# A convolution by short transforms: half of the first two products issued earlier, three bank pairs instead of four, row blocks in order

## The chip, the cores and the metric

The kernel runs on one core of one Trainium2 chip. The metric is device time in microseconds (us) of one execution. A core has these engines: TensorE (PE, matrix products into the accumulator memory PSUM; the loads of its stationary operand are shown as PEld), VectorE (DVE), ScalarE (ACT), GpSimd (POOL), and SyncE (SP), which here only issues transfers. Each engine works through its own list in order; semaphores order the lists among each other. PSUM has eight banks of 512 float columns.

## The reference

A convolution of width 3 along a sequence, from 1024 to 1024 channels, then a normalization with fixed mean and variance, then silu. Two sequences of 2048 positions, everything in bfloat16.

```python
B, S, C, K = 2, 2048, 1024, 3
xp = jnp.pad(x, ((0, 0), (1, 1), (0, 0)))
y = sum(jnp.einsum('bsc,cd->bsd', xp[:, k:k + S, :], w[k]) for k in range(K))
y = (y - mean) * (g * (1.0 / jnp.sqrt(var + 1e-5))) + b
return y * sigmoid(y)
```

## The kernel before

**Tiling.** Six output positions (R = 6) at a time are computed by eight products instead of eighteen. A block of eight inputs is transformed into eight points (NJ = 8); for each point, the transformed input is multiplied with a transformed weight; the eight results are combined into six rows. Points 0 and 7 (zero and infinity) use the raw taps 0 and 2 of w, the points in pairs (1, 2), (3, 4), (5, 6) use tiles u0, u1, u2 that POOL makes. A sequence has NB = 342 blocks; they are the columns of the products.

**Transforming the input.** x comes in 17 windows of 128 positions, each with the data of 21 blocks (WT = 21; the last has 6). PE multiplies a window, as stationary operand, with a constant matrix `rm` (for window 0 with `rm0`, a shifted copy that `first_matrix` makes through PSUM). One `t_job` (L322) does up to three of the eight channel tiles of two neighbouring windows: matmuls of 8 x 21 = 168 columns into two neighbouring banks, then one cast of both banks into `T_sb` in bfloat16, on ACT (L333) or on DVE (L335). Eight channel tiles take three jobs a pair of windows: tiles 0 to 2 and 3 to 5 (six matmuls, a cast of 128x1008 each), and 6 and 7 (four matmuls, 128x672). With the job of the 6-block window, which comes first (job 0), a sequence has 25 jobs. A planner in the Python code, which keeps a clock for each engine with a fixed cost and a cost per column, gives each cast to ACT or DVE, whichever would end first by its reckoning. `ahead` issues all jobs of the first sequence, on bank pairs 0, 2, 4, 6 in turn. `order` is the order of the windows: 16, then 2 to 15, then 0 and 1.

**Transfers.** SP's queue carries the windows of the first sequence in this order, with three half-width loads of w after the sixth, ninth and last window (`W0_AT`), then the second sequence's windows. There are 12 window buffers, so from the 13th window on a load waits for a job to release one.

**Units.** The work after that is 16 units, one for each of the 8 groups of 128 output channels and each sequence, on four banks each (0 to 3, then 4 to 7, and so on in turn). A product of a unit is eight matmuls, one for each channel tile, of 342 columns (L368). The first unit (`run_first`) multiplies points 0 and infinity first: product (3, 0), which is point 0 into bank 3, and (0, 7), point 7 into bank 0. Each needs all of `T_sb` for its point; ACT copies the results to `ends`. Then come points 1, 3, 2, 4, 5, 6. Between the matmuls of the first unit, `Between` issues the jobs of the second sequence at the counts of matmuls listed in `at`, on bank pairs 4-5, 6-7 and 1-2 in turn. Job q of this sequence uses `(4, 6, 1)[q % 3]`.

**The other units.** They multiply the inner points first; points 0 and 7 of a unit are added at the end (`first`, `last`), among the products of the next unit, each with the silu of one row (rows 0 and 5, L391). `silu_inner` does the four inner rows in two instructions. `rest` lists these three pieces with the place behind which each is issued. Where weights for a later unit are prepared, ACT also doubles a tile (`double_w`, L157) at the end of the unit. The results go to `yT`, are transposed by transfers and stored.

**Warm-up.** Before the first window is there, PE multiplies zeros (L74), `WARM` matmuls of 512 float columns.

Of the kernel before, what the change touches and what calls it, by code (L numbers as in the profile page):

```python
# [15 lines left out]
P = 128  # L16
R = 6
NJ = 8
W0_AT = (5, 8, 16)
EARLY = 23  # L20
XBUFS = 12
T_FIRST = 21500.0
WARM = 2
WT = 21

@with_exitstack
def kernel(
# [10 lines left out]
    nc = tc.nc  # L38
    B, S, C = x.shape
    D = w.shape[2]  # L40
    CT, DC = C // P, D // P
    NB = -(-S // R)
    NW = -(-NB // WT)
# [21 lines left out]
    ps = pspool.tile([P, 8, 512], FP32, name="ps")  # L65
    T_sb = [tpool.tile([P, CT, NJ, NB], BF16, name=f"T_sb{bi}") for bi in range(B)]
# [41 lines left out]
    clock = {"pe": 3500.0, "act": 0.0, "dve": 0.0, "dma": 3600.0}  # L108
# [3 lines left out]
    def ends(e, size):  # L112
        return max(clock[e], clock["pe"] + 100.0) + cost[e][0] * size + cost[e][1]
# [1 line left out]
    def busy(e, size):  # L115
        clock[e] = ends(e, size)

    order = [NW - 1] + list(range(2, NW - 1)) + [0, 1]
    xwin = {}

    def load_x(bi, wi):
# [86 lines left out]
    def prepare_first(dc):  # L208


        w0, w2 = raw[dc][:, 0], raw[dc][:, 2]
        g, f = (spool.tile([P, CT, P], BF16, name="w1x2") for _ in range(2))
        nc.gpsimd.tensor_scalar(f, w0, 4.0, 0.0, op0=ALU.mult, op1=ALU.add)
        for q, t, h in ((0, w0, w2), (1, g, w0)):
            if q:
                nc.gpsimd.tensor_scalar(g, w2, 4.0, 0.0, op0=ALU.mult, op1=ALU.add)
            sums[dc, q] = epool.tile([P, CT, P], FP32, name=f"e{q}")
            nc.gpsimd.tensor_tensor(sums[dc, q], t, h, op=ALU.add)

        def left():  # L220
            transform_w(dc, 0, (0,))
            double_w(dc, nc.scalar)
            transform_w(dc, 1, (0,))
            transform_w(dc, 0, (1,))
            transform_w(dc, 1, (1,))
            sums[dc, 2] = epool.tile([P, CT, P], FP32, name="e2")
            nc.gpsimd.tensor_tensor(sums[dc, 2], f, w2, op=ALU.add)
            transform_w(dc, 2)

        return left  # L230
# [40 lines left out]
    rm0 = consts.tile([P, NJ, WT], BF16, name="rm0")  # L271

    def first_matrix():

        v = ps[0:P - 1, 1, 256:256 + NJ * WT]
        nc.tensor.matmul(v, lhsT=ident[:, 1:P], rhs=rm.rearrange("p j n -> p (j n)"), start=True, stop=True)
        nc.scalar.copy(rm0[0:P - 1].rearrange("p j n -> p (j n)"), v)

    def params():

# [33 lines left out]
    def t_job(job, bank):  # L314
        wins, dst, n, c0, nct = job
        nb, size = len(wins), nct * NJ * n
        clock["pe"] = max(clock["pe"], wins[-1][1], bank_free.get(bank, 0.0))
        src = ps[:, bank:bank + nb, 0:size]
        v = src.rearrange("p b (c j n) -> p b c j n", j=NJ, n=n)
        for q, (xw, _, mat, rows) in enumerate(wins):  # L320
            for c in range(nct):
                nc.tensor.matmul(  # L322
                    v[:, q, c], lhsT=xw[0:rows, (c0 + c) * P:(c0 + c + 1) * P], rhs=mat[0:rows, :, 0:n],
                    start=True, stop=True,
                )
        dst = dst.rearrange("p c j (b n) -> p (c j) b n", b=nb)
        src = src.rearrange("p b (q n) -> p q b n", n=n)
        clock["pe"] += nb * size / 2.3
        e = min(("act", "dve"), key=lambda k: ends(k, nb * size))
        busy(e, nb * size)  # L330
        bank_free[bank] = clock[e] + 100.0
        if e == "act":
            nc.scalar.copy(dst, src)  # L333
        else:
            nc.vector.tensor_copy(dst, src)  # L335
# [8 lines left out]
    class Unit:  # L344
# [12 lines left out]
            self.low, self.mid, self.high = (ps[:, b0 + q:b0 + q + 2, lo:hi] for q in range(3))  # L357
            self.yT = yts[bi]

        def product(self, q, j, add, between):  # L360
            dc = self.dc
            nsl = slice(self.lo, self.hi)
            for ct in range(CT):
                if j == 0 or j == NJ - 1:
                    lhsT = raw[dc][:, 0 if j == 0 else 2, ct]
                else:
                    lhsT = wts[dc, (j - 1) // 2][:, (j - 1) % 2, ct]
                nc.tensor.matmul(  # L368
                    self.bank[q], lhsT=lhsT, rhs=T_sb[self.bi][:, ct, j, nsl],
                    start=not add and ct == 0, stop=ct == CT - 1, skip_group_check=add,  # L370
                )
                clock["pe"] += (self.hi - self.lo) / 2.35
                between()

        def copy(self, q, dst=None, by=None):
# [40 lines left out]
        def run_first(self, between, left, following):  # L416


            b0, b1, b2, b3 = self.bank
            sd = dpool.tile([P, 2, NB], FP32, name="sd")  # L420
            t = dpool.tile([P, 4, NB], FP32, name="t02")
            t0, t2 = t[:, 0:2], t[:, 2:4]
            ends = dpool.tile([P, 2, NB], FP32, name="ends")
            self.y23 = t1 = ypool2.tile([P, 2, NB], FP32, name="t1")
            left()
            self.product(3, 0, False, between)
            self.copy(3, dst=ends[:, 0])
            self.product(0, NJ - 1, False, between)
            self.copy(0, dst=ends[:, 1])
            clock["pe"] = max(clock["pe"], T_FIRST)  # L430
            self.product(3, 1, False, between)
            pa = self.copy(3)
            self.product(0, 3, False, between)
            pb = self.copy(0, by=4.0)
            self.product(3, 2, True, between)
            self.copy(3, dst=sd[:, 0])
            self.combine(sd[:, 1], pa, 2.0, b3, ALU.subtract)
            self.product(0, 4, True, between)
            self.combine(b1, b0, -2.0, pb)
            for d, a in ((t0, -0.0125), (t2, -0.2), (t1, -0.05)):  # L440
                self.combine(d, self.low, a, sd)
            nc.vector.tensor_tensor(t[:, 0::3], t[:, 0::3], ends, op=ALU.add)
            busy("dve", 2 * NB)
            first, second, third, fourth = following
            first()
            self.product(2, 5, False, between)
            pc = self.copy(2)
            between.rest()
            self.product(2, 6, True, between)
            self.combine(b3, b2, -0.5, pc)  # L450
            self.combine(self.low, self.high, -1.6, t0)
            self.combine(t1, self.high, -0.4, t1)
            self.combine(self.high, self.high, -0.1, t2)
            second()
            self.prepare = third, fourth
# [9 lines left out]
        def rest(self, between, last=5, first=6):  # L465


            return [
                (min(last, 5), self.silu_inner), (last, lambda: self.last(between)),
                (first, lambda: self.first(between)),  # L470
            ]

        def run(self, between, also=(), prepare=None, alone=False):

# [111 lines left out]
        if i in W0_AT:  # L586
            load_w(0, (0, 2, 1)[W0_AT.index(i)], 0)

    left = []

    def ahead(jobs, job_n):
        for job in jobs:
            t_job(job, job_n % 4 * 2)
            if job_n == 0:
                first_matrix()
            if job_n == 2:
                params()
            if job_n == 5:
                scales()
                left.append(prepare_first(0))  # L600
            job_n += 1

    ahead(t_jobs(0), 0)
# [5 lines left out]
    class Between:  # L609


        n = done = 0
        jobs = list(t_jobs(1))
        at = [8, 12, 14, 16, 18, 20, 22] + [22 + (6 * CT - 22) * (q + 1) // (EARLY - 7) for q in range(EARLY - 7)]

        def do(self):
            t_job(self.jobs[self.done], (4, 6, 1)[self.done % 3] if self.done < EARLY else (6, 4)[(self.done - EARLY) % 2])
# [11 lines left out]
    between = Between()  # L629
    seq = [(dc, bi) for dc in range(DC) for bi in range(B)]  # L630
    late = [nc.sync] * (S // R // P + 1) + [nc.gpsimd]
    before = prev = None
    for i, (dc, bi) in enumerate(seq[:-1]):
        unit = Unit(dc, bi, i % 2 * 4)
        if i == 0:
            unit.run_first(between, left[0], prepare_second(1))
        else:
            unit.run(
                between,
                prev.rest_first() if i == 1 else  # L640
                prev.rest(between, *((4, 5) if i >= len(seq) - 3 else (5, 4) if i == 2 else (5, 6))),
                2 if i == 2 else dc + 2 if bi == 1 and 0 < dc < DC - 2 else None,
                i == 1,
            )
        if i == 0:
            xwin_scope.close()
            olast = ctx.enter_context(tc.tile_pool(name="olast", bufs=3))
            wpools[1] = ctx.enter_context(tc.tile_pool(name="wpool1", bufs=1))
        if i in (0, 4, 8):
            for k in range(3):  # L650
                load_w(i // 4 + 1, k)
        if i == len(seq) - 2:
            prev.turn(olast, ((1, R), (0, 1)))
        elif prev:
            prev.turn()
        if before:
            before.store(late if i == len(seq) - 2 else ())
        before, prev = prev, unit
    before.store(late)
    dc, bi = seq[-1]  # L660
# [45 lines left out]
```

## Time and profile before

| | before |
|---|---|
| times of three runs | 188.25, 188.66, 190.04 us |
| profiled execution, its own time | 188.5 us |
| its span, first to last instruction | 186.7 us |
| PE busy | 177.0 us (95%), 1402 matmuls |
| DVE busy | 154.9 us (83%) |
| POOL busy | 146.1 us (78%) |
| ACT busy | 111.9 us (60%) |
| x and w reads, output writes | 14.82 MB read, 8.39 MB written |
| granted TensorE clock | 0.998 of full speed, mean of the span |

The page counts an instruction as busy from its start to its modelled end; PE's matmuls overlap, so the distance from one to the next is shorter than the duration given for one. Idle time is put down to what ended it ("<-DMA xw": a window of x arrived). "Issue" is time in which an engine waited for nothing that the profile shows.

### The profile page before, as it was taken

To read this page: it belongs to the slowest core of one execution; us is meant where nothing else is said; L and a number is where in the kernel's file an instruction comes from. 1 tells how busy PE (TensorE), PEld (TensorE's weight loads), DVE (VectorE), ACT (ScalarE), POOL (GpSimd) and SP (SyncE) were. 2 spreads that over 40 slices of the span, in tenths; PEclk is the share of its full clock that TensorE was granted. 3 is DMA by queue.
4 is the path that set the end of the run, shared out by engine and by line. 5 is a ranking of instruction groups with operands and counts; after the bars stand their busy time and mean duration, and the time that the engine had idled before them with its cause. 6 is when DMAs were issued, how large, how long until landed. Compare 5 with 4: busy or idle time off the path is not lost.

```text
span 186.7 us, 3721 instructions
## 1 busy us (share of the span) xinstructions
PE 177.0 (95%) x1402; PEld 125.0 (67%) x1402; DVE 154.9 (83%) x213; ACT 111.9 (60%) x182; POOL 146.1 (78%) x86
## 2 busy tenths in 40 slices
PE   6879999999999999999999999999999999999980
PEld 2658688776666666666666666666666666669980
DVE  5549667897979999999988998879988996769681
ACT  3789698689465565456545654565455555454790
POOL 3477999989998879999999999999999971021031
PEclk9999999999999999999999999999999999999999
DMA  5999999057607455798749667978596577979725
GB/s 168 315 351 334 381 388 232 4 151 193 123 4 142 102 109 130 196 187 198 150 109 210 115 136 201 202 178 167 115 199 117 123 79 163 181 140 167 162 62 112
DMA packets 86958, 31.72 MB, mean 170 GB/s; under 512 B 73542, under 2 KB 82778, under 8 KB 86940
## 3 DMA queue, kind: packets, MB, share of 16 engines
q1 hardware_dynamic: 85820, 31.24, 72.5%
q10 hardware_dynamic: 864, 0.21, 0.5%
q8 instruction: 11, 0.18, 0.4%
q0 software_dynamic: 256, 0.03, 0.2%
q14 instruction: 7, 0.06, 0.1%
HBM read 14.82 MB, written 8.39 MB: 124 GB/s over the span
## 4 chain that ended last, share of the span: by engine, by line
PE 83%; DMA 4%; DVE 4%; ACT 2%; SPq 2%; issue 1%; ACTq 0%; DVEq 0%
PE ps L368 77%; PE ps L322 5%; DVE T_sb L335 4%; DMA xw<-in_x_dram 3%; SPq L125 2%; DMA rows<-in_g_dram 1%; ACT yT L391 1%; ACT T_sb L333 1%; PE ps L534 1%; SPq L141 0%; ACTq L70 0%; DVEq L701 0%; ACT pc L379 0%; DVE sd L386 0%; DVE o L535 0%
## 5 line engine op out<-in xcount | busy, mean ns | idle before, releaser
L368 PE MATMUL ps<-T_sb,u 128*128 128x342 bf16 (+2 forms) x816 | 120.1, 299 | 0.5 <-ACT yT L391 0.5
L368 PEld LDWEIGHTS <-u 128*128 128x128 bf16 x816 | 76.7, 97 | 33.7 <-issue 0.7
L190 POOL TENSOR_TENSOR u<-e,w1x 128x1024 bf16<-128x1024 f32 x32 | 69.4, 2194 | 3.9 <-DVE e L171 2.5
L368 PE MATMUL ps<-T_sb,wch 128*128 128x342 bf16 (+2 forms) x272 | 43.0, 299 | 0.4 <-ACT T_sb L333 0.4
L391 ACT ACTIVATE yT<-ps,beta,scale 128x342 bf16<-128x342 f32 (+4 forms) x49 | 33.8, 721 | 11.9 <-PE ps L368 11.9
L190 POOL TENSOR_TENSOR u<-e,wch 128x1024 bf16<-128x1024 f32 x16 | 38.6, 2434 | 1.9 <-DMA wch<-in_w_dram 1.3
L386 DVE SCALAR_TENSOR_TENSOR t<-ps,sd 128x684 f32<-128x684 f32 (+2 forms) x51 | 39.1, 822 | 0.6
L368 PEld LDWEIGHTS <-wch 128*128 128x128 bf16 x272 | 25.6, 97 | 11.7 <-issue 0.7
L379 ACT COPY pc<-ps 128x342 f32<-128x342 f32 (+2 forms) x34 | 14.5, 427 | 30.1 <-PE ps L368 30.0
L335 DVE CAST T_sb<-ps 128x1008 bf16<-128x1008 f32 (+2 forms) x20 | 22.0, 1121 | 11.4 <-PE ps L322 11.2
L333 ACT CAST T_sb<-ps 128x1008 bf16<-128x1008 f32 (+2 forms) x30 | 24.9, 866 | 6.8 <-PE ps L322 6.6
L386 DVE SCALAR_TENSOR_TENSOR ps<-ps,t 128x684 f32<-128x684 f32 (+2 forms) x34 | 28.3, 832 | 0.6
L171 DVE SCALAR_TENSOR_TENSOR e<-wch 128x1024 f32<-128x1024 bf16 x12 | 27.2, 2263 | 0.0
L322 PE MATMUL ps<-rm,xw 128*128 128x168 bf16 (+2 forms) x272 | 24.8, 233 | 2.4 <-DMA xw<-in_x_dram 1.9
L322 PEld LDWEIGHTS <-xw 128*128 128x128 bf16 (+2 forms) x272 | 20.2, 97 | 8.3 <-DMA xw<-in_x_dram 3.0
L386 DVE SCALAR_TENSOR_TENSOR ps<-ps,pc 128x342 f32<-128x342 f32 (+2 forms) x34 | 16.8, 496 | 8.6 <-PE ps L368 7.5
L169 POOL TENSOR_TENSOR e<-wch 128x1024 f32<-128x1024 bf16 x7 | 16.9, 2409 | 0.0
L391 ACT ACTIVATE yT<-t,beta,scale 128x684 bf16<-128x684 f32 (+2 forms) x17 | 15.7, 926 | 0.0
L386 DVE SCALAR_TENSOR_TENSOR t<-ps,t 128x684 f32<-128x684 f32 (+2 forms) x17 | 13.9, 818 | 0.0
L576 POOL DMA_DIRECT2D out_dram<-o x2 | 1.4, 710 | 15.6 <-DMA o<-yT 15.6
L379 ACT COPY sd<-ps 128x342 f32<-128x342 f32 (+2 forms) x17 | 7.3, 429 | 9.7 <-PE ps L368 8.8
L381 ACT ACTIVATE pc<-ps 128x342 f32<-128x342 f32 (+2 forms) x17 | 7.5, 440 | 9.1 <-PE ps L368 6.8
(52 smaller groups left out, 61.3 us busy)
## 6 DMA issues: line engine op xcount, KB each, us to landing
xw<-in_x_dram SPq DMA_DIRECT2D x32, 256.0 KB
out_dram<-o SPq DMA_DIRECT2D x28, 192.0 KB
wch<-in_w_dram SPq DMA_DIRECT2D x9, 512.0 KB
out_dram<-o SPq DMA_DIRECT2D x14, 120.0 KB
wch<-in_w_dram SPq DMA_DIRECT2D x6, 256.0 KB
out_dram<-o SPq DMA_DIRECT2D x3, 128.0 KB
o<-yT SPq DMA_TRANSPOSE x15
out_dram<-o SPq DMA_DIRECT2D x12, 7.5 KB
```

Of the source, the lines that this page charges most:

```text
L125: nc.sync.dma_start(out=xw[0:hi - lo, :], in_=x[bi, lo:hi, :])
L169: eng.tensor_tensor(e, w0, w2, op=ALU.add)
L171: eng.scalar_tensor_tensor(out=e, in0=f, scalar=4.0, in1=h, op0=ALU.mult, op1=ALU.add)
L190: nc.gpsimd.tensor_tensor(wts[dc, q][:, i], sums[dc, q], o, op=(ALU.add, ALU.subtract)[i])
L322: nc.tensor.matmul(v[:, q, c], lhsT=xw[0:rows, (c0 + c) * P:(c0 + c + 1) * P], rhs=mat[0:rows, :, 0:n], start=True, stop=True,)
L333: nc.scalar.copy(dst, src)
L335: nc.vector.tensor_copy(dst, src)
L368: nc.tensor.matmul(self.bank[q], lhsT=lhsT, rhs=T_sb[self.bi][:, ct, j, nsl], start=not add and ct == 0, stop=ct == CT - 1, skip_group_che ...
L379: nc.scalar.copy(dst, self.bank[q])
L381: nc.scalar.mul(dst, self.bank[q], by)
L386: nc.vector.scalar_tensor_tensor(out=out, in0=in0, scalar=scalar, in1=in1, op0=ALU.mult, op1=op1)
L391: nc.scalar.activation(self.yT[:, rows, self.lo:self.hi], src, ACT.Silu, bias=beta[:, dc:dc + 1], scale=scale[:, dc:dc + 1])
```

## The change

- `order`: windows 16, 0, 1, ..., 15, for both sequences.
- `first_matrix` goes ahead of job 0; its copy is made by DVE instead of ACT. One warm-up matmul instead of two.
- From job 13 of the first sequence on, the jobs use the bank pairs 4-5, 6-7, 1-2 in turn (`(4, 6, 1)[job_n % 3]`); up to job 12, 0, 2, 4, 6 in turn as before.
- The first eight windows in order make up the first 168 columns, complete with job 12. Products (3, 0) and (0, 7) of the first unit are computed for these columns between jobs 13 and 18: six matmuls after job 13 and two after job 15 for the one, five after job 16 and three after job 18 for the other. `run_first` computes the other 174 columns where it computed 342.
- The second sequence's jobs 1 to 6 come at other counts of matmuls.
- `rest`: where the place of `first` comes before the places of the other two, the list is turned round. That holds in the third unit alone, where the last product and row 5's silu of the second unit now come ahead of its inner silus.
- `T_FIRST`, a lower bound for the planner's clock, goes from 21500 to 21000.

```diff
-T_FIRST = 21500.0
-WARM = 2
+T_FIRST = 21000.0
+HALF = 8
+WARM = 1
...
-    order = [NW - 1] + list(range(2, NW - 1)) + [0, 1]
+    order = [NW - 1] + list(range(NW - 1))
...
-        nc.scalar.copy(rm0[0:P - 1].rearrange("p j n -> p (j n)"), v)
+        nc.vector.tensor_copy(rm0[0:P - 1].rearrange("p j n -> p (j n)"), v)
...
-        def product(self, q, j, add, between):
+        def product(self, q, j, add, between, cols=None, cts=range(CT), part=None):
+
             dc = self.dc
-            nsl = slice(self.lo, self.hi)
-            for ct in range(CT):
+            nsl = cols or slice(self.lo, self.hi)
+            dst = ps[:, self.b0 + q, nsl]
+            for ct in cts:
...
                 nc.tensor.matmul(
-                    self.bank[q], lhsT=lhsT, rhs=T_sb[self.bi][:, ct, j, nsl],
-                    start=not add and ct == 0, stop=ct == CT - 1, skip_group_check=add,
+                    dst, lhsT=lhsT, rhs=T_sb[self.bi][:, ct, j, nsl],
+                    start=not add and part != 1 and ct == cts[0], stop=part != 0 and ct == cts[-1],
+                    skip_group_check=add,
                 )
-                clock["pe"] += (self.hi - self.lo) / 2.35
+                clock["pe"] += (nsl.stop - nsl.start) / 2.35
...
-            self.product(3, 0, False, between)
+            late = slice(HALF * WT, NB)
+            self.product(3, 0, False, between, late)
             self.copy(3, dst=ends[:, 0])
-            self.product(0, NJ - 1, False, between)
+            self.product(0, NJ - 1, False, between, late)
...
                 (first, lambda: self.first(between)),
-            ]
+            ][::1 if first >= min(last, 5) else -1]
...
-    left = []
+    left, one = [], Unit(0, 0, 0)
+    half = {
+        13: (3, 0, (3, 4, 5, 6, 7, 0), 0), 15: (3, 0, (1, 2), 1),
+        16: (0, NJ - 1, (3, 4, 5, 6, 7), 0), 18: (0, NJ - 1, (0, 1, 2), 1),
+    }
 
     def ahead(jobs, job_n):
         for job in jobs:
-            t_job(job, job_n % 4 * 2)
             if job_n == 0:
                 first_matrix()
+            t_job(job, job_n % 4 * 2 if job_n < HALF // 2 * 3 + 1 else (4, 6, 1)[job_n % 3])
...
+            if job_n in half:
+                q, j, cts, part = half[job_n]
+                one.product(q, j, False, lambda: None, slice(0, HALF * WT), cts, part)
             job_n += 1
...
-        at = [8, 12, 14, 16, 18, 20, 22] + [22 + (6 * CT - 22) * (q + 1) // (EARLY - 7) for q in range(EARLY - 7)]
+        at = [8, 16, 16, 16, 20, 21, 22] + [22 + (6 * CT - 22) * (q + 1) // (EARLY - 7) for q in range(EARLY - 7)]
```

More of the change, by code (lines that the diff above doesn't have):

```diff
@@ L633 @@
     for i, (dc, bi) in enumerate(seq[:-1]):
-        unit = Unit(dc, bi, i % 2 * 4)
+        unit = Unit(dc, bi, i % 2 * 4) if i else one
         if i == 0:
```

## The prediction

> **What bounds the kernel now.** I read the busy time by stretch first, to see where TensorE (PE) is short of work at all. Columns: stretch, its length, then busy us and instructions of PE, PE's weight loads, VectorE (DVE), ScalarE (ACT), GpSimd (POOL); clock, DMA share, GB/s.
>
> ```profile
> 9.00:13.49 4.49, 2.86 (x32) 2.25 (x33) 2.33 (x3) 4.01 (x6) 3.49 (x7) 1.00 1.10 349
> 13.49:19.31 5.82, 5.24 (x61) 4.48 (x62) 4.92 (x5) 5.21 (x8) 4.36 (x4) 1.00 1.10 340
> 19.31:38.20 18.89, 18.62 (x193) 14.92 (x193) 13.50 (x15) 14.08 (x21) 18.73 (x10) 1.00 0.74 237
> 38.20:181.00 142.80, 142.34 (x1062) 98.62 (x1061) 127.91 (x166) 83.11 (x142) 115.28 (x55) 1.00 0.72 147
> ```
>
> From 38.20 to 181.00 PE idles for 0.46 us in 142.8. So whatever shifts the start of that stretch shifts the end by as much, and nothing there gives it back. Up to 13.49 PE waits for x windows (DMA share about 1). From 13.49 to 19.31 it is neither full nor starved by DMA; DVE and ACT are busy there for 4.92 and 5.21 us of 5.82. The chain of waits (start, length, work) says who sets the pace:
>
> ```profile
> 14.35 0.93 DVE T_sb L335
> ...
> 16.73 0.61 PE ps L322 x6
> 17.34 0.02 issue
> 17.36 1.91 ACT T_sb L333 x2
> ...
> 19.31 1.44 PE ps L368 x8
> ...
> 30.86 1.22 DVE T_sb L335
> 32.09 0.04 issue
> 32.13 0.61 PE ps L322 x6
> 32.74 0.02 issue
> 32.76 1.21 DVE T_sb L335
> ```
>
> At 14 to 19 us the casts of transformed windows out of PSUM carry the chain, then the first product. At 30.86 the reader sees the row that matters most below: a DVE cast, PE refilling the same pair of banks, the next DVE cast. From cast to cast that is 32.76 - 30.86 = **1.90 us**. It is the period whenever a DVE cast and its refill alternate on one pair. The timeline of single instructions gives the unit prices.
>
> ```profile
> 13.49 0.61 PE L322 MATMUL ps<-rm,xw 128*128 128x168 bf16 x6 [0.30 <-DMA xw<-in_x_dram]
> 14.35 1.21 DVE L335 CAST T_sb<-ps 128x1008 bf16<-128x1008 f32 x1 [1.58 <-PE ps L322]
> 18.61 1.21 DVE L335 CAST T_sb<-ps 128x1008 bf16<-128x1008 f32 x1
> 19.15 0.74 ACT L333 CAST T_sb<-ps 128x672 bf16<-128x672 f32 x1
> 19.31 0.60 PE L368 MATMUL ps<-T_sb,wch 128*128 128x342 bf16 x3 [0.45 <-ACT T_sb L333]
> ```
>
> One 168-column record alone lasts 0.25, six 0.61: a step of (0.61 - 0.25)/5 = 0.072 us. One 342-column record lasts 0.31, three 0.60: a step of 0.145. The casts of job 14 and job 23 are those at 14.35 and 18.61: three pairs of windows in 4.26 us, 1.42 a pair.
>
> **The start.** One warm-up matmul less frees PE about 1.85 us earlier (four records of warm-up in 3.71 us). The first matrix goes ahead of job 0, its copy moves from ACT (0.30) to DVE (between that and the 0.56 of a 384-column DVE cast); DVE is idle from 3.64 to 6.61. Row blocks 0 and 1 merely change places with others in the load order; sizes and queue stay. All of it lies before 9.59, where PE has waited 0.96 us for the seventh window. I take 0; if that window came at once, the cover were gone and the gain at most 0.96.
>
> A rule of the Trainium skill speaks against the missing warm-up: "TensorE: Matmul & The Clock Gate", Part 1, says that the array runs at half clock until it has been busy for about 3.4 us. The profile shows a granted clock of 1.00 from the first slice on, so no run here shows that state at the start.
>
> **The sixteen half products.** The diff issues 16 matmuls of 168 columns between jobs 13 and 18, and leaves 16 of 174 columns where there were 16 of 342. The later cost falls from 0.145 to 0.145 x 174/342 = 0.074 each, 16 x 0.071 = 1.14 us off the path. In front, 61 matmuls x 0.072 = 4.4 of the 5.82 us after 13.49 are needed, so 1.4 us is free for 16 x 0.072 = 1.15. By PE's time alone they fit. But their results stay in banks 0 and 3, and that is the price:
>
> **The ring of three.** From job 13 on, jobs go round three bank pairs (4-5, 6-7, 1-2) instead of four. A pair of windows is also three jobs. So the first job of each pair always meets banks 6-7, the second banks 1-2, the third 4-5. The planner's arithmetic (fixed plus per-column cost, earliest end wins), carried through with the diff's terms, gives ACT, DVE, ACT for each of the last four pairs; for the kernel before, the same arithmetic gives exactly the engines in the trace. So DVE casts jobs 14, 17, 20, 23, all in banks 1-2: the 1.90 us cycle. PE, in order, waits for those banks, and all later jobs queue behind it.
>
> Job 14 is ready after the six half products of job 13: 14.35 + 6 x 0.072 = 14.79. Then 16.69, 18.59, 20.49, and the last cast ends at 20.49 + 1.21 = 21.70; before, 18.61 + 1.21 = 19.82. **1.88 us later.** Nothing else is slower than 1.90 a pair: ACT needs 1.51 (0.90 + 0.61 from start to start), PE at most 21 x 0.072 = 1.51, the windows came in for 1.42 a pair.
>
> Now the first product. Channel tiles 0 to 2 can go at 20.58, when job 24's matmuls are issued; tile 3 waits for job 23's cast, 21.75; five steps of 0.074 give 22.12. Before, it ended at 20.69: +1.43. From there to the unit's third product it takes 0.32 (job 0) + 1.16 (jobs 1 to 3) in both, plus 8 x 0.145 = 1.16 before and 0.59 after. Net at that point: 1.43 - 0.57 = **+0.86**.
>
> The bounds: if the ring costs nothing and only the 0.44 of half products delays the casts, 0.44 - 1.02 = -0.58, where 1.02 = 1.88 - 0.86 is what the shorter products return. If PE's and ACT's queueing adds a tenth to each cycle, 3 x 0.19 more, +1.43. I take +0.86, because the 1.90 row is this very pattern.
>
> **The second sequence's jobs.** Jobs 1 to 3 now come in one bunch at the 16th matmul, jobs 4 to 6 at the 20th to 22nd. Carrying on with the same durations, job 4 waits 0.16 us for job 1's banks (DVE cast until 24.88), job 7 0.10, job 8 0.07: **+0.33**, bounds 0 and 0.66 (all covered; each twice as long). ACT's doubling of w1, at 19.76 before, shifts behind the later casts; POOL needs its result two tiles ahead of PE, which leaves over 2 us of cover; without that it would cost the 1.9 us of the shift. The x loads that wait for released windows go out up to 1 us later; their queue was full until 29 us, so this is hidden.
>
> **Row 5's silu first in the third unit.** This takes away PE's only stall after 38 us:
>
> ```profile
> 53.88 0.96 ACT L391 ACTIVATE yT<-t,beta,scale 128x684 bf16<-128x684 f32 x1
> 54.74 1.44 ACT L391 ACTIVATE yT<-ps,beta,scale 128x684 bf16<-128x684 f32 x2
> 56.06 1.06 ACT L157 ACTIVATE w1x<-wch 128x1024 bf16<-128x1024 bf16 x1
> 57.59 0.45 ACT L379 COPY pc<-ps 128x342 f32<-128x342 f32 x1 [0.47 <-PE ps L368]
> 56.23 5.97 PE L368 MATMUL ps<-T_sb,u 128*128 128x342 bf16 x40 [0.46 <-ACT yT L391]
> ```
>
> PE could go on at 54.44 + 8 x 0.145 = 55.60 and goes on at 56.23: 0.63 to gain. But ACT now idles until row 5's product is done, 54.64, and everything behind moves back: row 5 until 55.16, the two inner silus (0.86, 0.81 from start to start) until 56.83, the doubling until 57.79, and only then the copy of the next unit's first product, done at 58.24. The product that adds into that bank would start at 55.60 + 16 x 0.145 = 57.92 and waits until 58.28. **0.63 - 0.36 = -0.27**; bounds -0.63 (the copy is in time) and +0.1 (it comes half a microsecond later than I add up). So a stall of 0.46 becomes one of about 0.36, two products later.
>
> **Sum.** 0 + 0.86 + 0.33 - 0.27 = +0.92. The profiled execution took 188.5 (span 186.7, 1.8 around it); the median of the runs shown is 188.66, near enough the same. **189.4 us.**
>
> **Rivals.** *The ring is no bound* (other side). If PE refills in time and the casts of jobs 13 to 24 keep their 1.42 us a pair, the change gains: 0.44 - 1.02 - 0.27 = -0.85, 187.65; with the full 0.63 of the third unit 187.3. It turns at the period c where 0.44 + 3(c - 1.42) = 1.02 - 0.33 + 0.27 = 0.96, that is c = 1.59. For it: PE has 1.4 us free there. Against it: the 1.90 row. Chance 0.16.
>
> *The delay is absorbed.* If the stretch from 19.31 to 38.20 is bound by something that arrives at a fixed time, a later start costs nothing: 188.5 - 0.27 = 188.2. For it: POOL is busy for 18.73 of its 18.89 us, making the tiles PE needs. Against it: the last tile of that unit is done at 33.7, before its use after 36, and no wait of PE on POOL shows. Chance 0.11.
>
> *The three-bank cycle also takes over the second sequence.* At 30 to 37 us it already does now and then; if the bunch starts it ten microseconds sooner, each of seven pairs loses another 0.16: 189.4 + 1.1 = 190.5. Against it: PE has products to issue between the jobs there. Chance 0.13.
>
> *The clock stays at half while the windows are transformed.* Then the 77 matmuls left at 13.7 take 77 x 0.145 = 11.2, until 24.9 instead of 20.6: about +4, 193.7. Chance 0.03. The Trainium skill's page on TensorE and its clock gate, Part 1, would make it so until PE has been busy for one whole window; by its 3.4 us, as an estimate, that would be over before 13 us.
>
> **How the numbers follow.** 0.57 is left for my forecast, whose own range is 188.8 to 190.1 (the bounds above, not all at once). With the rivals, 187.6 to 191.0 leaves out the best end of the first and the clock. A measurement of this kernel can tell about 1% from no change: 186.8 and 190.5. Faster than that needs more than any case but the ends of two: 0.04. Slower: the clock, half or so of the third rival and the far end of mine, 0.17. Same: 0.79.
>
> **What would show it.** Right: four DVE casts in that stage 1.9 us apart, the last ending near 21.7; the first product's fourth matmul waiting on it; the second sequence's job 0 near 22.1; no stall of PE at the fourth unit's start but one on ACT's copy two products on; all after 40 us shifted by about 0.9. Wrong: casts closer than 1.6 us; two DVE casts in one pair of windows, so another split between the engines; matmuls of 168 columns in steps of 0.14; PE waiting for x after 14 us.

## The result and the profile after

The changed kernel takes 189.76 us (median; 189.06 to 191.15), the kernel before 188.70. The ratio is **1.0063**, with a 95% interval of 1.0048 to 1.0078: slower by 0.9 to 1.5 us. The prediction said 189.4, 0.92 above the profiled execution of before. The profiled execution of the changed kernel has a span of 187.6 us against 186.7, and a time of its own of 189.36 against 188.5.

The busy time by stretch of the changed kernel, with the same columns as before; the second stretch follows the later work:

```profile
13.49:19.31 5.82, 5.29 (x68) 4.88 (x68) 3.15 (x3) 4.93 (x7) 3.89 (x3) 1.00 1.09 338
39.50:182.00 142.50, 142.32 (x1062) 98.57 (x1060) 128.26 (x166) 82.99 (x142) 115.27 (x55) 1.00 0.70 147
```

In the first stretch VectorE (DVE) is down from 4.92 to 3.15 us. It was busy for most of that stretch and now waits, although there is as much to cast. The chain of waits says for what:

```profile
14.79 1.22 DVE T_sb L336
...
16.05 0.61 PE ps L323 x6
...
16.68 1.22 DVE T_sb L336
...
20.47 1.22 DVE T_sb L336
...
21.73 0.54 PE ps L371 x5
```

A cast, a refill of the same two banks by PE, the next cast: this loop carries the chain from 14.79 to 21.69, three rounds of 1.89 us. Before, such a loop stands in the chain only from 30.86 us on. The timeline of PE shows what it costs the first product:

```profile
21.73 0.54 PE L371 MATMUL ps<-T_sb,wch 128*128 128x174 bf16 x5 [0.78 <-DVE T_sb L336]
22.20 0.38 PE L323 MATMUL ps<-rm,xw 33*128 33x48 bf16 x8
...
39.42 1.76 PE L371 MATMUL ps<-T_sb,u 128*128 128x342 bf16 x11
```

Job 0 of the second sequence, which marks the end of the first product, is at 22.20 (before: 20.69), the first unit's last product at 39.42 (before: 38.18). The third and fourth unit, on ACT and PE:

```profile
55.89 0.64 ACT L395 ACTIVATE yT<-ps,beta,scale 128x342 bf16<-128x342 f32 x1 [0.66 <-PE ps L371]
...
58.08 1.04 ACT L158 ACTIVATE w1x<-wch 128x1024 bf16<-128x1024 bf16 x1
59.02 0.43 ACT L383 COPY pc<-ps 128x342 f32<-128x342 f32 x1
55.69 3.65 PE L371 MATMUL ps<-T_sb,u 128*128 128x342 bf16 x24
59.51 1.75 PE L371 MATMUL ps<-T_sb,u 128*128 128x342 bf16 x11 [0.18 <-ACT pc L383]
```

PE runs on past row 5's silu, 24 matmuls from 55.69, and could go on at 55.69 + 24 x 0.145 = 59.17. It goes on at 59.51, when ACT's copy behind the doubling is done: 0.63 us of stall have become 0.34.

### The profile page after: what moved, and what is told of

Read it like the earlier page. It is cut to its first block, busy times and chain, and to the rows that moved or that the text cites. A ratio compares the mean times of both kernels' runs of the same rounds, so it can differ in the third digit from the quotient of the medians.

```text
span 187.6 us, 3748 instructions
## 1 busy us (share of the span) xinstructions
PE 177.7 (95%) x1416; PEld 127.0 (68%) x1416; DVE 154.9 (83%) x213; ACT 112.7 (60%) x182; POOL 145.9 (78%) x86
## 4 chain that ended last, share of the span: by engine, by line
PE 87%; DVE 7%; ACT 2%; issue 1%; DVEq 0%; ACTq 0%
PE ps L371 77%; PE ps L323 9%; DVE T_sb L336 5%; ACT T_sb L334 1%; PE ps L539 1%; DVE rm L104 0%; ACT yT L395 0%; DVE zeros L73 0%; DVEq L713 0%; DVE m L90 0%; DVE sd L390 0%; DVE f L92 0%; DVE f L95 0%; PE ps L277 0%; PE ps L283 0%
## 5 line engine op out<-in xcount | busy, mean ns | idle before, releaser
L371 PE MATMUL ps<-T_sb,wch 128*128 128x342 bf16 (+4 forms) x288 | 43.4, 292 | 0.8 <-DVE T_sb L336 0.8
L371 PEld LDWEIGHTS <-wch 128*128 128x128 bf16 x288 | 26.6, 97 | 11.6 <-issue 0.9
L336 DVE CAST T_sb<-ps 128x1008 bf16<-128x1008 f32 (+2 forms) x19 | 21.4, 1136 | 12.6 <-PE ps L323 12.6
L334 ACT CAST T_sb<-ps 128x1008 bf16<-128x1008 f32 (+2 forms) x31 | 25.7, 861 | 7.2 <-PE ps L323 6.9
L323 PE MATMUL ps<-rm,xw 128*128 128x168 bf16 (+2 forms) x272 | 26.8, 244 | 2.5 <-DVE T_sb L336 0.9
L323 PEld LDWEIGHTS <-xw 128*128 128x128 bf16 (+2 forms) x272 | 21.9, 102 | 8.0 <-issue 4.5
```

Source lines behind the costliest of these rows:

```text
L323: nc.tensor.matmul(v[:, q, c], lhsT=xw[0:rows, (c0 + c) * P:(c0 + c + 1) * P], rhs=mat[0:rows, :, 0:n], start=True, stop=True,)
L371: nc.tensor.matmul(dst, lhsT=lhsT, rhs=T_sb[self.bi][:, ct, j, nsl], start=not add and part != 1 and ct == cts[0], stop=part != 0 and ct = ...
```

## The experiments

My theory: the loop of cast and refill on one pair of banks makes the delay. Its rival: the half products themselves, the start or the new counts do. Each time below is a median; each ratio is to the kernel before on the same chip. One thing has to be taken out when traces are compared: the windows of x do not arrive at the same time in every execution. Job 13's second window let PE go on at 13.49 in the kernel before, and at 13.14 to 14.07 in executions of kernels whose list up to there is the same. So I measure in each trace from job 14's cast to the first unit's last product: **23.83 us before** (14.35 to 38.18) and 24.63 in the changed kernel, plus the 0.44 of half products that stand ahead of its job 14: **25.07, 1.24 more**. The measure has a spread of its own: four traces of kernels with the list of the kernel before up to that point (before, the two runs on the silu and the doubling, and the last one below) have 23.83, 23.97, 23.93 and 23.81.

**The ring without the half products.** In `ahead`, and in `run_first`:

```diff
-            if job_n in half:
-                q, j, cts, part = half[job_n]
-                one.product(q, j, False, lambda: None, slice(0, HALF * WT), cts, part)
...
-            late = slice(HALF * WT, NB)
+            late = slice(0, NB)
```

> The changed kernel without the half products: three bank pairs from job 13 on stay, and run_first computes all 342 columns of points 0 and infinity. Theory (the ring makes the delay): VectorE's casts of jobs 14, 17, 20 and 23 still start 1.90 us apart, now from 14.35, the last ends at 14.35 + 3 x 1.90 + 1.21 = 21.26; the sequence-2 job 0 comes near 22.0, and the full-width second product adds 0.57, so about 0.4 above the changed kernel: 190.1 us, 1.4 above the kernel before. Rival (the sixteen half products delay the casts, the ring is free): casts 1.42 apart, the last ends at 19.8 as in the kernel before, total about 188.7.

190.41 us, ratio 1.0089 (1.0071 to 1.0106). VectorE's casts of that stage:

```profile
16.48 1.21 DVE L336 CAST T_sb<-ps 128x1008 bf16<-128x1008 f32 x1 [0.69 <-PE ps L323]
18.37 1.21 DVE L336 CAST T_sb<-ps 128x1008 bf16<-128x1008 f32 x1 [0.69 <-PE ps L323]
20.26 1.21 DVE L336 CAST T_sb<-ps 128x1008 bf16<-128x1008 f32 x1 [0.69 <-PE ps L323]
```

1.89 apart, each waiting 0.69 us for the refill, with no half product anywhere. From job 14's cast (14.58) to the last product of the unit (40.12) it is 25.54, 1.71 more than before. So the ring makes the delay without them, and the half products give back 25.54 - 25.07 = 0.47 of it.

**Four pairs.** As the last one, and in `ahead`:

```diff
-            t_job(job, job_n % 4 * 2 if job_n < HALF // 2 * 3 + 1 else (4, 6, 1)[job_n % 3])
+            t_job(job, job_n % 4 * 2)
```

> The changed kernel without the half products and with four bank pairs for all 25 jobs; window order, one warm-up matmul, the counts and the third unit's order stay as changed. Theory: the casts are those of the kernel before (14.35 and 18.61 for jobs 14 and 23, end 19.8). What is left is the counts (+0.15 to +0.33) and the third unit (-0.29): 188.7 us, no difference to the kernel before. Rival (the start counts after all: half-rate matmuls before 8.5 us, the new order of windows): casts of job 13 and later start late, 189.2 or more.

189.31 us, ratio 1.0024 (1.0001 to 1.0047). The stage is as the theory has it:

```profile
14.49 1.21 DVE L336 CAST T_sb<-ps 128x1008 bf16<-128x1008 f32 x1 [1.33 <-PE ps L323]
18.72 1.21 DVE L336 CAST T_sb<-ps 128x1008 bf16<-128x1008 f32 x1
```

Three pairs of windows in 4.23 us, 1.41 a pair, and 24.09 us to the last product, 0.26 more than before. This differs from the run before it in the ring alone, and takes 1.45 us off that stretch. The parts add up to what the change did there: 1.45 - 0.47 + 0.26 = 1.24. But the whole time fell short: 189.31 instead of 188.7. In this trace PE waits later on, most of all for VectorE at 81.64 (0.28 us idle), and there are smaller waits at 45, 52 and 59 us, of which the changed kernel has only the last. Both come up again below.

**ScalarE and VectorE in turn.** In `t_job`, for jobs 13 to 24 of the first sequence:

```diff
         e = min(("act", "dve"), key=lambda k: ends(k, nb * size))
+        if job_n is not None and job_n >= 13:
+            e = ("act", "dve")[(job_n - 13) % 2]
```

> The changed kernel with ScalarE and VectorE taking turns at the casts of jobs 13 to 24 (ScalarE the odd jobs), so that banks 1-2 are emptied by VectorE, ScalarE, VectorE, ScalarE. Theory (the cycle is cast plus refill on one pair): the casts from banks 1-2 come 1.90 us after a VectorE cast and 1.69 after a ScalarE cast (1.00 + 0.05 + 0.44 + 0.20); the last cast ends near 21.4 instead of 21.68, and ScalarE's shorter casts save 0.3 to 0.45 in all: 189.35 us. Rival (three pairs cost the same whoever casts): 189.76.

189.51 us, ratio 1.0049 (1.0031 to 1.0068). The times alone don't tell this from the changed kernel. The trace does: banks 1-2 are now cast by VectorE at 14.83, then

```profile
16.72 1.00 ACT L336 CAST T_sb<-ps 128x1008 bf16<-128x1008 f32 x1 [0.95 <-PE ps L323]
18.48 1.21 DVE L338 CAST T_sb<-ps 128x1008 bf16<-128x1008 f32 x1 [0.54 <-PE ps L323]
20.37 1.00 ACT L336 CAST T_sb<-ps 128x1008 bf16<-128x1008 f32 x1 [0.91 <-PE ps L323]
```

1.89 after a VectorE cast, 1.76 after a ScalarE cast. The unit's last product comes 24.72 after job 14's cast with the 0.44 added, 0.35 sooner than in the changed kernel. Some of it is lost again later: PE waits for VectorE before 81.51, by the steps of its matmuls 0.25 us (0.04 in the changed kernel).

**Two warm-up matmuls.** `WARM = 2` in the changed kernel.

> The changed kernel with two warm-up matmuls as before. Theory: 168-column matmuls step 0.072 from 5.5 us on instead of 0.14 until 8.5, and PE then waits about 0.9 us for the window that comes at 9.54 instead of 0.21: no change, 189.76 us, cast of job 14 at 14.79 in both. Rival (the half rate at the start delays windows and weights): job 14's cast earlier by 0.2 or more, 189.5 or less.

189.84 us, ratio 1.0065 (1.0047 to 1.0082): no difference, as the theory had it. The way there was another. In this trace the 168-column matmuls still step by 0.14 us until 7.3 us, and PE idles 0.32 us, not 0.9, for the window that comes at 9.86. So the run shows that the second warm-up matmul is worth nothing here; it doesn't compare a start without half rate with one that has it. Job 14's cast was at 15.14, later and not earlier, as the windows came late in this execution; to the last product it is the same 25.07.

**The counts of before.** In the changed kernel:

```diff
-        at = [8, 16, 16, 16, 20, 21, 22] + ...
+        at = [8, 12, 14, 16, 18, 20, 22] + ...
```

> The changed kernel with the second sequence's jobs at the counts of the kernel before (8, 12, 14, 16, 18, 20, 22 instead of 8, 16, 16, 16, 20, 21, 22). Theory: the bunch of jobs 1 to 3 costs 0.15 to 0.33 us by refills that wait for casts: 189.5 us. Rival (the new counts suit the shorter products): 189.8 or more.

Ratio 1.0054 (1.0037 to 1.0070), median 189.94: unclear by the times, with the median on the rival's side (189.8 or more). In the trace it is 24.92 to the last product, 0.15 less than in the changed kernel, the lower end of what was expected. PE's waits ahead of the single jobs say where it comes from. The changed kernel waits 0.15 us ahead of job 4 (until 25.02), 0.09 ahead of job 7 (26.71) and 0.14 ahead of job 8 (27.57); the kernel before has only 0.08 ahead of job 8. With the old counts the wait ahead of job 4 stays (0.14), and the other two are back at 0.08 together. The 0.15 doesn't reach the end of this trace: before 82.26 PE waits 0.19 us for VectorE.

**The silu's order alone**, in the kernel before:

```diff
-            ]
+            ][::1 if first >= min(last, 5) else -1]
```

> The kernel before with the third unit's new order alone: the last product and row 5's silu ahead of the inner silus. Theory (0.63 us of stall goes, 0.34 comes back because ScalarE's doubling is now ahead of the fourth unit's first copy): span shorter by 0.29, 188.4 us. Rival (the whole stall goes): shorter by 0.63, 188.1 us.

188.46 us, ratio 0.9983 (0.9965 to 1.0002). The stall is 0.34 us, as in the changed kernel: PE waits from 58.64 to 58.98. The time agrees with -0.29 and doesn't exclude 0 or the rival's -0.63; the trace excludes the rival.

**The doubling moved too.** In `run`, ahead of `behind(5)`, and left out at the end of that unit:

```diff
+            if prepare == 2:
+                idle(act_work)
             behind(5)
...
-                idle(act_work)
+                if prepare != 2:
+                    idle(act_work)
```

> As the kernel before with the third unit's new order, and ScalarE's doubling of a weight tile moved ahead of row 5's silu, into the time in which ScalarE waits for that row's product (53.9 to 54.7). Theory: row 5's silu ends near 55.5, the inner silus near 57.1, the copy of the fourth unit's first product near 57.5, before the product that adds into its bank could start (57.92): both stalls go, shorter by 0.63, 188.1 us. Rival (the silus are late anyway): as with the new order alone, 188.4.

188.37 us, ratio 0.9980 (0.9961 to 0.9999): half of what was expected. Both stalls are gone, PE runs through from 55.13. In their place there is a new one, 0.37 us by the steps of the matmuls before it:

```profile
81.05 1.32 PE L368 MATMUL ps<-T_sb,wch 128*128 128x342 bf16 x8 [0.21 <-DVE ps L386]
```

**Point 0 in the gap behind job 24.** With the last edit, `WARM`, the counts and the four pairs as before, windows in order:

```diff
-        13: (3, 0, (3, 4, 5, 6, 7, 0), 0), 15: (3, 0, (1, 2), 1),
-        16: (0, NJ - 1, (3, 4, 5, 6, 7), 0), 18: (0, NJ - 1, (0, 1, 2), 1),
+        24: (3, 0, range(CT), None),
...
-            self.product(0, NJ - 1, False, between, late)
+            self.product(0, NJ - 1, False, between)
```

> A version meant to be faster than both: four bank pairs for all jobs, two warm-up matmuls, the counts of the kernel before, windows in order; only point 0 gets its first 168 columns early, as eight matmuls behind job 24, where PE stood still from 18.70 to 19.31 and bank 3 is free (its last cast ends at 18.69); run_first computes the other 174 columns of point 0 and all 342 of point infinity. The doubling stands ahead of row 5's silu as in the run on that. Theory: the gap takes 8 x 0.072 = 0.58; the first product ends at 19.87 + 5 x 0.074 = 20.24 instead of 20.69, and the third unit gives 0.63: 188.7 - 0.45 - 0.63 = 187.6 us. Rival (an early result in bank 3 costs as the ring did, or the gap is not free): 188.1 or more.

188.43 us, ratio 0.9975 (0.9956 to 0.9994), not 187.6. In front it works: 23.48 us from job 14's cast (14.45) to the last product (37.93), 0.35 less than before and 0.33 less than the smallest of the four traces with the old list. But at 80 us:

```profile
79.69 0.80 DVE ps L390
...
80.52 93.23 PE ps L371 x656
```

This is the chain of waits of that version. PE waits for VectorE's last combination of the fifth unit, 0.60 us by the profile, 0.76 by the steps. VectorE works there with hardly a pause from 55 us on. In the kernel before, the same combination ended at 80.32, and PE needed it at 80.61. So from 56.23, where its stall ends, to 81 us PE looked free of waits, and still only **0.3 us** lay between it and VectorE's list.

That list in turn follows POOL's. VectorE's first sum for the weights in this stretch, in this version and in the kernel before, with the POOL instruction beside which it starts:

```profile
58.17 2.13 POOL L191 TENSOR_TENSOR u<-e,wch 128x1024 bf16<-128x1024 f32 x1
58.54 2.84 DVE L172 SCALAR_TENSOR_TENSOR e<-wch 128x1024 f32<-128x1024 bf16 x1
```

```profile
58.01 2.14 POOL L190 TENSOR_TENSOR u<-e,wch 128x1024 bf16<-128x1024 f32 x1
58.77 2.45 DVE L171 SCALAR_TENSOR_TENSOR e<-wch 128x1024 f32<-128x1024 bf16 x1
```

VectorE starts 0.23 us sooner than before, but the sum ends 1.08 us after POOL's instruction in both, and in every trace of this case; a sum that starts when POOL has none under way takes 1.2 us (1.22 at 123.24 in the kernel before). POOL is 0.16 later here, so the combination ends at 80.47, where it ended at 80.32 before. PE could have gone on 0.85 us sooner than before and goes on 0.09 sooner. Why the sum ends behind POOL's instruction, no run tells. The longer sum is also in the traces with four pairs (2.84), with the engines in turn (2.66) and with the old counts (2.60), and in each of them PE waits longer for VectorE at about 82 us than in the changed kernel (sum 2.44, wait 0.04).

**The sum moved behind the combinations.** To test that, with the last version and with the doubling alone:

```diff
-            idle(dve_work)
+            if (self.dc, self.bi) != (2, 0):
+                idle(dve_work)
...
             behind(6)
+            if (self.dc, self.bi) == (2, 0):
+                idle(dve_work)
```

> As the version with point 0 in the gap behind job 24, and in the fifth unit VectorE's sum for the weights (2.04 us) moved behind that unit's combinations, where it stood ahead of the last four. The traces so far show VectorE without a pause from 55.6 to 81 us there, and PE waiting 0.60 us for its last combination at 80.52 in that version. Theory (VectorE's list up to 81 us is a second floor, 0.3 us under the kernel before, and took back what PE had gained): the combinations end 2 us earlier, no wait of PE near 81, 0.6 less: 187.8 us. Rival (the gain was lost elsewhere, in windows that come late): no change, 188.4.

> The kernel before with the third unit's new order, the doubling ahead of row 5's silu, and the fifth unit's sum moved in the same way; no early products. Theory: the 0.21 us that PE waited at 81.05 goes, and the whole 0.63 of the third unit reaches the end: 188.1 us. Rival: 188.4 as without the moved sum.

With the early products 188.15 us, ratio 0.9961 (0.9937 to 0.9986), where 187.8 was expected; without them 188.06, ratio **0.9959** (0.9937 to 0.9981), as expected. The wait at 81 us is gone in both. In its new place the sum takes 1.25 us instead of 2.05, as POOL's instruction is nearly over when it starts. In the second, the time from the first unit's last product (37.82) to PE's last group (180.96) is 143.14 us, against 143.76 before (38.18 to 181.94): 0.62, the whole of the third unit. In the first it is 144.03 (37.95 to 181.98), 0.89 more: 0.67 before 45.59 and 0.22 before 52.77, by the steps of PE's matmuls. POOL, ACT and PE:

```profile
20.24 2.13 POOL L191 TENSOR_TENSOR u<-e,wch 128x1024 bf16<-128x1024 f32 x1 [2.69 <-DMA wch<-in_w_dram]
...
44.15 1.06 ACT L240 ACTIVATE w1x<-wch 128x1024 bf16<-128x1024 bf16 x1 [0.86 <-POOL e L246]
45.59 5.97 PE L371 MATMUL ps<-T_sb,u 128*128 128x342 bf16 x40 [0.51 <-ACT pc L383]
```

The last half-width load of w arrived at 20.24, and POOL's whole list for the first two units shifted; ACT waited for POOL, and PE for ACT's copy behind that. The run with four pairs had the load at 20.44, which goes with its waits at 45 and 52 us. The changed kernel itself had it at 20.34 and the run with the engines in turn at 20.08; there PE came later, and no wait at 45 or 52 us shows. The other eight traces had it at 18.70 to 19.59. Why it comes in two groups no run tells. The late four are all of kernels with the windows in order; but four others of that order had the load early, as had all four with the old order, so the order is a suspect and no more. It may also have cost the run with four pairs part of its 189.31. Whether the early product is worth its 0.35 us (0.18 in the second trace) when the load comes early wasn't settled: the two versions measure the same.

## Why the prediction was right, and where it was off

- **The start, 0.** Right, and nearer the edge than I said. In the trace of the changed kernel 168-column matmuls step by 0.14 us until 8.6 us, and by 0.072 from there. The same 23 of them, in the kernel before and in the changed one:

```profile
6.62 2.01 PE L322 MATMUL ps<-rm,xw 128*128 128x168 bf16 x23
```

```profile
6.49 2.84 PE L323 MATMUL ps<-rm,xw 127*128 127x168 bf16 x23
```

  PE's wait for the window at 9.54 hid it, with 0.21 us left of 0.96. That is the rule of the Trainium skill, "TensorE: Matmul & The Clock Gate", Part 1, and the trace agrees: half rate at first, full rate after several microseconds of work. The granted clock in the profile says 1.00 all through, so it doesn't show this state; that no run here shows it, as the prediction had it, was wrong. The second warm-up matmul doesn't make sure of the full rate either: of the four traces of kernels with the old list up to there, two step by 0.072 from about 5.5 us on, and the runs on the silu and the doubling step by 0.14 until 7.3 and 6.6. Nothing was lost by it: PE still waited 0.8 us or more for the window that follows.
- **The ring of three, +0.86.** Right step by step: casts predicted for 14.79, 16.69, 18.59, 20.49, seen at 14.79, 16.68, 18.57, 20.47. The distances are what the mechanism gives; that the first cast came at 14.79 to the hundredth is luck, as the windows came in this execution when they had come before: the same jobs had that cast at 15.14 and 15.44 in the runs with two warm-up matmuls and with the old counts. Job 0 came at 22.20 instead of 22.12, and the third product started at 24.29 against 23.33, +0.96.
- **The counts, +0.33.** The sum of 0.96 and what followed is 1.24 at the unit's last product, so 0.28. Right job by job: 0.16, 0.10 and 0.07 us predicted ahead of jobs 4, 7 and 8, seen 0.15, 0.09 and 0.14, of which the kernel before had 0.08. But the run with the old counts puts only 0.15 of it down to them; the wait ahead of job 4 comes with them or without, so it goes with the ring or the half products.
- **The third unit, -0.27.** Measured 0.63 - 0.34 = -0.29, by the mechanism I gave: a stall that moves to ACT's copy behind the doubling.
- **The sum, +0.92.** 1.24 - 0.29 = 0.95 in the traces, a ratio of 1.0063 in the times. The third unit's 0.29 reached the end because it is just under the 0.3 us at 81 us: PE waited 0.04 us there. The prediction didn't look for that bound.
- **"Nothing there gives it back."** Right for a later start, wrong as a general statement. Where PE gains, 0.3 us below it there is VectorE's list to 81 us, which follows POOL's, and there is POOL's list itself when the w load comes late. The prediction's rival on the other side, 187.65 with a ring that costs nothing, didn't have these bounds; whether that time could have been reached no run tells.

## What to carry to other kernels

To size a ring of buffers, add up the time for which one buffer is taken. With three bank pairs for groups of three jobs, each pair is cast and refilled once a group, one after the other, so with VectorE casting a group took 1.89 us, 1.21 of cast and the rest for the refill; with four pairs a group took 1.41. Who casts which pair mattered less: with the engines in turn it was 1.89 and 1.76 in turn. Holding two banks back for early results cost 1.45 us of waiting, and the early results gave 0.47 of it back. And before costing a gain, look how far each other engine's list ends ahead of the engine that sets the pace: a bound that shows no wait in the trace can be 0.3 us away.

## What was not expected of the hardware

The windows of x that end PE's wait near 13.5 us arrived at 13.14 to 14.07 in executions with the same list up to there, more than most effects studied here. Distances from job 14's cast on differ by 0.16 us between traces with the same list, and the single waits of PE behind the first unit's third product by 0.01; medians of twelve runs tell neither. And VectorE's sums for the weights last from 1.2 to 3.2 us, by how much of a POOL instruction is left when they start: in all twelve traces they end 1.08 us or more behind it. It goes the other way too: the POOL instruction that starts at 123.30 in the kernel before, 0.06 us behind such a sum, takes 3.15 us instead of 2.13.
